# The second feed-forward layer's first product, computed block-wise by Strassen's seven products

## Chip, cores, metric

One core of a Trainium2 chip runs the whole program. The metric is device time in microseconds (us), the median of the runs shown.

## What is computed

Inputs are q, k, v of shape (4, 8, 576, 64) and two pairs of weights, 512 x 2048 and 2048 x 512, all float32. A retention step (attention with a decaying mask) makes 2304 tokens of 512 features; two feed-forward layers follow.

```
scores = scale * q @ k.T;  ret = scores * Dmat;  x = ret @ v        # 2304 x 512
h = x @ w_in;  g = max(h, 0) + log1p(exp(-abs(h)));  x = g @ w_out  # first phase
h = x @ w_in;  r = max(h, 0);  g = r * r;            x = g @ w_out  # second phase
```

## The kernel before

TensorE multiplies float32r operands. To reach float32 precision, each operand is split into a high part (a rounding cast on ScalarE) and a low part (the rest, a subtraction on VectorE), and each product is made of three matmuls: high by high, low by high, high by low.

The tokens are cut into five blocks per phase, of 512 or 384 tokens (`TILES`, `TILES2`, L25 and L26). In a block the loop goes over 16 slices `f` of 128 hidden features. One step of it is: `g1` (L306 to L320), the first product, 12 matmuls that put 128 features by `n` tokens into one of two PSUM tiles `ph`; the nonlinearity on ScalarE and VectorE (`softplus_a` and `softplus_b` in the first phase, `relu2_a` and `relu2_b`, L349 to L358, in the second); `split_g` (L360), the high and low part of the result; and `g2` (L370), the second product, which adds into PSUM tiles `acc` that live for a whole block. `g2` of a step is issued two steps after its `g1` (L512), so the elementwise chain has two steps of TensorE work to hide behind. In the second phase `g2` holds 128 tokens stationary and moves 512 output columns, so it has 9 matmuls per step for 384 tokens and 12 for 512.

Weights arrive as raw 64-bit words, one 512 KB load for each 128-row slice (`load_w`, L100), are put together as float32 on ScalarE (L125, L126) and VectorE (L130) and split into high and low parts (L139, L140). `pump` and `pump_step` issue this work between the steps: the first phase's 32 slices during block 0 (`weights`, L483), the second phase's during the last block of the first phase and the first of the second (L518 to L525). Retention runs chunk by chunk (64 tokens) between the steps of blocks 0 to 3 (`attend`, L469); each chunk is loaded `LOADS` chunks ahead. The output of the first phase goes to DRAM (`x2d`) and is loaded again block by block (`load_x`).

All loads and stores are issued from SyncE's queue. The order on each engine is set by a scheduler at build time, which may issue independent instructions in another order than the code has; only the start (L436 to L463) is written out by hand.

Of the kernel before, what the change touches and what calls it, by code (L numbers as in the profile page):

```python
# [19 lines left out]
SCN = 9  # L20
LOADS = 4
STAGES = 3
EARLY = 8

TILES = ((0, 512), (512, 384), (896, 512), (1408, 512), (1920, 384))  # L25
TILES2 = ((0, 384), (384, 512), (896, 512), (1408, 512), (1920, 384))  # L26

# [7 lines left out]
def kernel(  # L35
# [19 lines left out]


    nc = tc.nc
    NT, DM = out.shape
# [14 lines left out]
    stage = ctx.enter_context(tc.tile_pool(name="stage", bufs=STAGES))  # L73
    cvt = ctx.enter_context(tc.tile_pool(name="cvt", bufs=3))
    xs = ctx.enter_context(tc.tile_pool(name="xs", bufs=1))
# [16 lines left out]
    mask = cst[CN:P, C_MASK:C_MASK + CN].unsqueeze(1).to_broadcast([CN, H, CN])  # L92
    x2d = dram.tile([KD, P, NT], F32, name="x2d")


# [14 lines left out]

    def split_w(phase, kind, f):

        t = staged.pop((kind, f))  # L120
        y, up, low = t.bitcast(F32)[:, :, 1], t[:, :, 1], t[:, :, 0]
        ct = cvt.tile([P, DM], U32, tag="ct", name="ct")
# [12 lines left out]
        y = ct.bitcast(F32)  # L135
        pool = wts if f < EARLY else late_wts[0]
        hi = pool.tile([P, DM], F32R, tag=f"{kind}h{f}", name=f"{kind}h{f}")
        lo = pool.tile([P, DM], F32R, tag=f"{kind}l{f}", name=f"{kind}l{f}")
# [6 lines left out]
    for phase, (wi, wo) in enumerate(((w1_in, w1_out), (w2_in, w2_out))):  # L145
        for f in range(KF + 2):
            if f < KF:
                items.append((phase, wi, "wi", f))
            if f >= 2:
                items.append((phase, wo, "wo", f - 2))  # L150
    n_load = [0]
    n_split = [0]

    def pump_load(upto):
        while n_load[0] < min(upto, len(items)):
            _, src, kind, f = items[n_load[0]]
            load_w(src, kind, f)
            n_load[0] += 1
# [3 lines left out]
    def pump_step():  # L162

        if not splitting:
            m = n_split[0]
            if m == len(items):
                return
            pump_load(m + 1)
            splitting.append(split_w(items[m][0], items[m][2], items[m][3]))
            n_split[0] += 1  # L170
        if next(splitting[0]):
            splitting.clear()
            pump_load(n_split[0] + STAGES)

# [110 lines left out]

    def split_x(raw, phase, n):

        xop.clear()
        for kk in range(KD):
            h, l = x_hi()[:, kk, :n], x_lo()[:, kk, :n]  # L290
            if phase == 0:
                r = raw[:, :n // CN, kk]
                h, l = (a.rearrange("p (m b) -> p m b", b=CN) for a in (h, l))
            else:
                r = raw[:, kk, :n]
            if kk % 2 == 0:
# [8 lines left out]

    def g1(phase, key, f, n):  # L306
        ph = ps_h.tile([P, 512], F32, tag="h", name="ph")
        wh, wl = w_hi[phase, "wi", f], w_lo[phase, "wi", f]
        todo, rest = [], []
# [38 lines left out]

    def relu2_a(key, n):  # L349
        r = ew.tile([P, 512], F32, tag="e", name="r", bufs=3)[:, :n]  # L350
        nc.scalar.activation(out=r, in_=hps.pop(key)[:, :n], func=AF.Relu)  # L351
        tmp[key] = r

    def relu2_b(key, n):
        r = tmp.pop(key)
        g = ew.tile([P, 512], F32, tag="l", name="g")[:, :n]
        nc.vector.tensor_tensor(out=g, in0=r, in1=r, op=ALU.mult)  # L357
        tmp[key] = g  # L358

    def split_g(key, n):  # L360
# [8 lines left out]

    def g2(phase, key, f, n, begin, end):  # L370
        h, l = gg.pop(key)
        wh, wl = w_hi[phase, "wo", f], w_lo[phase, "wo", f]
        n_out = KD if phase == 0 else n // P
        if begin:
            for j in range(n_out):
                acc[j] = ps_acc.tile([P, 512], F32, tag="at", name="acc")
        for j in range(n_out):
            c = slice(j * P, (j + 1) * P)
            if phase == 0:
                o = acc[j][:, :n]  # L380
                todo = [(wh[:, c], h[:, :n]), (wh[:, c], l[:, :n]), (wl[:, c], h[:, :n])]
            else:
                o = acc[j]
                todo = [(h[:, c], wh), (h[:, c], wl), (l[:, c], wh)]
            for m, (a, x) in enumerate(todo):
                nc.tensor.matmul(o, lhsT=a, rhs=x, start=(begin and m == 0), stop=(end and m == 2))  # L386

    def drain(phase, t0, n):
        for j in range(KD if phase == 0 else n // P):
            w = n if phase == 0 else DM  # L390
            if j % 2 == 0:
                o = cvt.tile([P, 512], F32, tag="ct", name="xo")
            else:
                o = ew.tile([P, 512], F32, tag="l", name="xo")
            if j % 2 == 0:
                nc.scalar.copy(o[:, :w], acc[j][:, :w])
            else:
                nc.vector.tensor_copy(o[:, :w], acc[j][:, :w])
            if phase == 0:
                nc.sync.dma_start(out=x2d[j, :, t0:t0 + n], in_=o[:, :w])  # L400
            else:
                nc.sync.dma_start(out=out[t0 + j * P:t0 + (j + 1) * P, :], in_=o)

    def load_x(t0, n):
        raw = xs.tile([P, KD, 512], F32, tag="xr", name="xr")
        nc.sync.dma_start(
            out=raw[:, :, :n], in_=x2d[:, :, t0:t0 + n].rearrange("k p n -> p k n")
        )
        return raw


    blocks = [(0, t0, n) for t0, n in TILES] + [(1, t0, n) for t0, n in TILES2]
    steps = [(b, f) for b in range(len(blocks)) for f in range(KF)]
    last_b = len(TILES) - 1

    need = [(t0 + n) // CN for t0, n in TILES]

    x_next = [None]

# [63 lines left out]
    def weights(j):  # L483

        first = (2, 2, 2, 3)[:j + 1]
        return min(len(items) // 2, 2 + int(sum(first) + 1.9 * (j + 1 - len(first))))

    def run_g2(j):
        b, f = steps[j]
        ph, t0, n = blocks[b]  # L490
        g2(ph, j, f, n, f == 0, f == KF - 1)
        if f == KF - 1:
            drain(ph, t0, n)

    for j, (b, f) in enumerate(steps):
        ph, t0, n = blocks[b]
        g1(ph, j, f, n)
        if ph == 0:
            softplus_a(j, n)
        else:  # L500
            relu2_a(j, n)
        if j == 0:
# [3 lines left out]
        if j >= 1:  # L506
            split_g(j - 1, blocks[steps[j - 1][0]][2])
        if ph == 0:
            pump(max(0, weights(j) - n_split[0]))
        if ph == 0:  # L510
            attend(b, f)
        if j >= 2:  # L512
            run_g2(j - 2)
        if ph == 0:
            softplus_b(j, n)
        else:
            relu2_b(j, n)
        if b in (last_b, last_b + 1):  # L518
            base = f + KF * ph
            goal = len(items) // 2 + max(int(0.6 * (base + 1)), 2 * (base - KF) + 5)  # L520
            while n_split[0] < min(goal, len(items)):
                _, _, kind, wf = items[n_split[0]]
                if wf + (1 if kind == "wi" else 3) > base:
                    break
                pump(1)  # L525
        if f == KF - 1 and b + 1 < len(blocks):
            split_x(x_next[0] if b >= last_b else x_raw.pop(b + 1), *blocks[b + 1][::2])
            if last_b <= b + 1 < len(blocks) - 1:
                x_next[0] = load_x(*blocks[b + 2][1:])
    j = len(steps)  # L530
    split_g(j - 1, blocks[-1][2])
    run_g2(j - 2)
    run_g2(j - 1)


# [73 lines left out]
```

## Time and profile before

| | us |
|---|---|
| median of 3 runs (lowest, highest) | 894.03 (892.5, 896.06) |
| the profiled execution | 897.41 |
| its span in the trace | 895.6 |
| TensorE matmuls busy in that span | 880.3 |
| VectorE busy | 480.0 |
| ScalarE busy | 426.0 |

The profile is of one execution, 3.38 us above the median; 1.8 us of it lie outside the span. Matmul records are modelled to their end and overlap, so matmuls are best priced by the distance between their starts.

### The profile page before, as it was taken

What the parts mean: (1) busy time and instruction counts of PE and PEld (TensorE: products, weight loads), DVE (VectorE), ACT (ScalarE), POOL (GpSimd) and SP (SyncE); (2) the same over time, 40 slices, a digit from 0 to 9 for tenths busy, and PEclk for the clock granted to TensorE, in tenths of its full rate; (3) what the DMA queues carried; (4) which work ended last, traced back from release to release, by engine and by line L of the source; (5) the groups of instructions that cost most, each with busy time, mean ns of one, the idle gap of its engine ahead of it and who ended that gap; (6) DMA issues with size and microseconds to landing.
All of it is one profiled execution on the core that took longest, in us unless ns stands there. A gap on an engine that the chain in (4) does not pass through costs nothing.

```text
span 895.6 us, 13279 instructions
## 1 busy us (share of the span) xinstructions
PE 880.3 (98%) x5462; PEld 756.4 (84%) x5462; DVE 480.0 (54%) x788; ACT 426.0 (48%) x751; POOL 9.6 (1%) x13
## 2 busy tenths in 40 slices
PE   7799999999999999999999999999999999999998
PEld 7677887999888888888999999888888888888997
DVE  2589998666756575556776777322432243223322
ACT  2479997444544444444795697222222222222222
POOL 2100000000000000000000000000000000000000
PEclk9899999999999999999999999999999999999999
DMA  9957674211211112000530673200010011000100
GB/s 226 211 173 222 197 207 132 80 48 48 84 48 48 27 44 71 2 1 2 194 123 1 203 224 103 83 1 0 29 66 1 0 36 48 1 1 0 48 1 36
DMA packets 36012, 68.69 MB, mean 77 GB/s; under 512 B 2928, under 2 KB 21488, under 8 KB 35952
## 3 DMA queue, kind: packets, MB, share of 16 engines
q1 hardware_dynamic: 35952, 67.85, 25.9%
q8 instruction: 43, 0.70, 0.3%
q14 instruction: 17, 0.14, 0.0%
HBM read 58.40 MB, written 9.44 MB: 76 GB/s over the span
## 4 chain that ended last, share of the span: by engine, by line
PE 91%; ACT 3%; DMA 3%; DVE 1%; SPq 1%; issue 0%; POOL 0%
PE ph L317 43%; PE acc L386 43%; PE st L239 3%; PE po L261 2%; DMA ch<-in_kv_dram 1%; DMA cst<-in_consts_dram 1%; DMA wi_raw<-in_moe_w_in_dram 1%; PE st L245 1%; DVE ct L130 0%; ACT wi_raw L126 0%; ACT e L332 0%; ACT woh L139 0%; ACT wi_raw L125 0%; ACT e L331 0%; ACT l L333 0%
## 5 line engine op out<-in xcount | busy, mean ns | idle before, releaser
L317 PE MATMUL ph<-xh,wih 128*128 128x512 f32 (+1 forms) x640 | 238.1, 372 | 1.9 <-ACT wih L139 1.0
L317 PE MATMUL ph<-xh,wil 128*128 128x512 f32 (+1 forms) x640 | 237.8, 372 | 0.0
L317 PE MATMUL ph<-xl,wih 128*128 128x512 f32 (+1 forms) x640 | 158.7, 369 | 0.0
L317 PEld LDWEIGHTS ph<-xh,wih 128*128 128x128 f32 x640 | 121.0, 189 | 20.1 <-ACT wih L139 1.4
L317 PEld LDWEIGHTS ph<-xh,wil 128*128 128x128 f32 x640 | 121.0, 189 | 16.7
L317 PEld LDWEIGHTS ph<-xl,wih 128*128 128x128 f32 x640 | 117.9, 189 | 15.3
L386 PE MATMUL acc<-gh,woh 128*128 128x512 f32 (+1 forms) x320 | 120.5, 376 | 0.0
L386 PE MATMUL acc<-gh,wol 128*128 128x512 f32 (+1 forms) x320 | 117.8, 368 | 0.0
L386 PE MATMUL acc<-gl,woh 128*128 128x512 f32 (+1 forms) x320 | 117.7, 368 | 0.0
L386 PE MATMUL acc<-woh,gl 128*128 128x512 f32 x288 | 112.6, 391 | 0.0
L386 PE MATMUL acc<-wol,gh 128*128 128x512 f32 x288 | 112.6, 391 | 0.0
L357 DVE TENSOR_TENSOR g<-r 128x512 f32<-128x512 f32 (+1 forms) x80 | 50.9, 636 | 114.8 <-ACT r L351 112.0
L386 PE MATMUL acc<-woh,gh 128*128 128x512 f32 x288 | 112.0, 389 | 0.0
L351 ACT ACTIVATE r<-ph 128x512 f32<-128x512 f32 (+1 forms) x80 | 44.2, 552 | 131.1 <-PE ph L317 131.1
L365 DVE TENSOR_TENSOR gl<-g,gh 128x512 fp32r<-128x512 f32 (+1 forms) x80 | 51.0, 638 | 101.7 <-ACT gh L364 101.7
L364 ACT CAST gh<-g 128x512 fp32r<-128x512 f32 (+1 forms) x80 | 46.2, 578 | 113.9 <-PE acc L386 106.7
L364 ACT CAST gh<-e 128x512 fp32r<-128x512 f32 (+1 forms) x80 | 46.1, 576 | 104.8 <-DVE e L344 77.4
L338 DVE SCALAR_TENSOR_TENSOR e<-e 128x512 f32<-128x512 f32 (+1 forms) x80 | 51.0, 638 | 65.5 <-ACT l L333 64.7
L365 DVE TENSOR_TENSOR gl<-e,gh 128x512 fp32r<-128x512 f32 (+1 forms) x80 | 51.0, 637 | 36.5 <-ACT gh L364 36.0
L331 ACT ACTIVATE e<-ph 128x512 f32<-128x512 f32 (+1 forms) x80 | 44.3, 554 | 53.3 <-PE ph L317 52.5
L386 PEld LDWEIGHTS acc<-gh,woh 128*128 128x128 f32 x320 | 60.0, 188 | 8.7
L386 PEld LDWEIGHTS acc<-gh,wol 128*128 128x128 f32 x320 | 60.1, 188 | 7.8
(48 smaller groups left out, 1026.5 us busy)
## 6 DMA issues: line engine op xcount, KB each, us to landing
wi_raw<-in_moe_w_in_dram SPq DMA_DIRECT2D x32, 512.0 KB, 4.6
wo_raw<-in_moe_w_out_dram SPq DMA_DIRECT2D x32, 512.0 KB, 4.2
ch<-in_qk_t_dram SPq DMA_DIRECT2D x36, 256.0 KB, 4.3
ch<-in_kv_dram SPq DMA_DIRECT2D x36, 256.0 KB, 4.7
out_dram<-xo SPq DMA_DIRECT2D x18, 256.0 KB, 2.0
x2d<-xo SPq DMA_DIRECT2D x12, 256.0 KB, 2.3
xr<-x2d SPq DMA_DIRECT2D x3, 1024.0 KB, 5.0
x2d<-xo SPq DMA_DIRECT2D x8, 192.0 KB, 2.0
```

The source lines that it names most:

```text
L239: nc.tensor.matmul(pb[HI, h, :], lhsT=kk[LO, h, :], rhs=qp[LO, h, :], start=True, stop=True, skip_group_check=True,)
L245: nc.tensor.matmul(st[LO, h, :], lhsT=kk[HI, h, :], rhs=sv[HI, h, :], start=c % SCH == 0 and h == 0, stop=True, skip_group_check=True,)
L261: nc.tensor.matmul(po[(LO, HI)[h % 2], h // 2, :], lhsT=sv[rows, h, :], rhs=qp[rows, h, :], start=True, stop=True, skip_group_check=True,)
L317: nc.tensor.matmul(ph[:, :n], lhsT=a, rhs=x, start=(j == 0), stop=(j == len(todo) - 1))
L331: nc.scalar.activation(out=e, in_=ph[:, :n], func=AF.Abs)
L338: nc.vector.scalar_tensor_tensor(out=e, in0=e, scalar=-2.0, in1=e, op0=ALU.add, op1=ALU.mult)
L351: nc.scalar.activation(out=r, in_=hps.pop(key)[:, :n], func=AF.Relu)
L357: nc.vector.tensor_tensor(out=g, in0=r, in1=r, op=ALU.mult)
L364: nc.scalar.copy(h[:, :n], g)
L365: nc.vector.tensor_tensor(out=l[:, :n], in0=g, in1=h[:, :n], op=ALU.subtract)
L386: nc.tensor.matmul(o, lhsT=a, rhs=x, start=(begin and m == 0), stop=(end and m == 2))
```

## The change

The first product of the second phase is no longer computed slice by slice over blocks of 512 or 384 tokens. The weight matrix is taken in pairs of hidden slices (`p` and `p + 8`) and halves of the 512 inner features, which makes a 2 x 2 block matrix A; the tokens are taken in three pairs of 384, which with the inner halves makes a 2 x 2 block matrix B. Strassen's scheme (Winograd's form) gets the four blocks of A B from seven block products instead of eight. Each block product is 6 matmuls of 384 columns. The sums of weight blocks (S) are made once, during blocks 1 to 3 of the first phase, written to DRAM (`s2d`, 8 pairs of 7 operands of 256 KB) and streamed back for each of the three token pairs through five slots (`load_s`). The sums of token blocks (T) are made on VectorE and ScalarE (`build_t`), for the first pair during the last block of the first phase, for the others during the pair before. The products are combined on VectorE from two PSUM buffers (`px`, `py`, `pz` share them). The second product is unchanged in its arithmetic and is cut into pieces of 3 matmuls, which are issued between the block products. `LOADS` goes from 4 to 3 and `cvt` from 3 to 6 buffers. The core of the diff:

```
-LOADS = 4
+LOADS = 3
...
+A11, A12, S2, S4, S3, S1, A22 = range(7)
+PRODUCTS = (A11, S2, A12, S3, S1, A22, S4)
+T_SLOTS = 10
+S_SLOTS = 5
...
+    def store_s(p, first, src):
+        n = src.shape[1] // (KH * P)
+        h, l = (new_ct(F32R)[:, :n * KH * P] for _ in range(2))
+        nc.scalar.copy(h, src)
+        nc.vector.tensor_tensor(out=l, in0=src, in1=h, op=ALU.subtract)
+        for part, o in enumerate((h, l)):
+            nc.sync.dma_start(
+                out=s2d[p, first:first + n, :, part].rearrange("o p c -> p o c"),
+                in_=o.bitcast(F32).rearrange("p (o c) -> p o c", o=n),
+            )
+
+    def split_s(p):
+        cts = []
+        for f in (p, p + NP):
+            t = staged.pop(("wi", f))
+            cts.append(new_ct())
+            yield from words(t, cts[-1])
...
+        store_s(p, A11, top)
+        yield
+        store_s(p, A22, a22)
+        yield
+        nc.vector.tensor_tensor(out=a22, in0=a21, in1=a22, op=ALU.add)
+        nc.vector.tensor_tensor(out=a21, in0=a11, in1=a21, op=ALU.subtract)
+        nc.vector.tensor_tensor(out=a11, in0=a22, in1=a11, op=ALU.subtract)
+        nc.vector.tensor_tensor(out=a12, in0=a12, in1=a11, op=ALU.subtract)
+        yield
+        store_s(p, S3, bot)
+        yield
+        store_s(p, S2, top)
+        yield True
...
+    def build_t(i):
+        k = i % 7
+        if k == 1:
+            nc.vector.tensor_tensor(out=raw(0, 0), in0=raw(0, 1), in1=raw(0, 0), op=ALU.subtract)
+            nc.vector.tensor_tensor(out=t2(), in0=raw(1, 1), in1=raw(0, 0), op=ALU.subtract)
+        elif k == 3:
+            nc.vector.tensor_tensor(out=raw(0, 1), in0=raw(1, 1), in1=raw(0, 1), op=ALU.subtract)
+        elif k == 5:
+            nc.vector.tensor_tensor(out=raw(1, 0), in0=raw(1, 0), in1=t2(), op=ALU.subtract)
+        src = (raw(0, 0), t2(), raw(1, 0), raw(0, 1), raw(0, 0), raw(1, 0), raw(1, 1))[k]
+        t = t_slot(i)
+        nc.scalar.copy(t[:, 0], src)
+        nc.vector.tensor_tensor(out=t[:, 1], in0=src, in1=t[:, 0], op=ALU.subtract)
...
+    def finish(b, p, i, j, c, done=None):
...
+        nc.scalar.copy(h, g)
+        nc.vector.tensor_tensor(out=l, in0=g, in1=h, op=ALU.subtract)
+        for m in range(MH):
+            pieces.append((b, p, i, j, m, (h, l)))
...
+        count = (2, 2, 2, 1, 2, 2, 1)
+        skip = 5
...
+                    if b + 1 < NB and p in (3, 4, 5) and k == 2:
+                        build_t((b + 1) * 7 + p - 3)
+                    if b + 1 < NB and p == NP - 1 and k < 4:
+                        build_t((b + 1) * 7 + 3 + k)
+                    if b == 0 and k in (0, 3):
+                        if n_split[0] < len(items) and not (p >= 4 and k == 3):
+                            pump(1)
+                    load_s((b * NP + p) * 7 + k + 1 + S_SLOTS)
...
+                product(b, p, 0, px, True)
+                nc.scalar.copy(s1, px)
+                after(0)
+                product(b, p, 1, py, True)
+                nc.vector.tensor_tensor(out=u2, in0=s1, in1=py, op=ALU.add)
+                after(1)
+                product(b, p, 2, px, False)
+                nc.scalar.activation(out=r, in_=px, func=AF.Relu)
+                later.append(lambda: finish(b, p, 0, 0, None, r))
+                after(2)
+                product(b, p, 3, py, False)
+                nc.vector.tensor_tensor(out=u3, in0=s1, in1=py, op=ALU.add)
+                after(3)
+                product(b, p, 4, pz, True)
+                c22 = add(u3, pz)
+                later.append(lambda: finish(b, p, 1, 1, c22))
+                after(4)
+                product(b, p, 5, py, False)
+                c21 = add(s1, py)
+                later.append(lambda: finish(b, p, 1, 0, c21))
+                after(5)
+                product(b, p, 6, pz, False)
+                c12 = add(u2, pz)
+                later.append(lambda: finish(b, p, 0, 1, c12))
+                after(6)
...
+        if 1 <= b < last_b:
+            total, i = 9 * NP, (b - 1) * KF + f
+            while n_steps[0] < min(total, -(-total * (i + 1) // (KF * (last_b - 1) - 2))):
+                pump_step()
+                n_steps[0] += 1
+        if b == last_b:
...
+            if f >= 4 and f % 2 == 0:
                 pump(1)
+            for i in range(7):
+                if f == GROUP * (i // 2) + GROUP + 1 + i % 2:
+                    build_t(i)
```

`after(k)` first runs the finish that stands in `later`, then issues `count[k]` pieces, then the extra work shown. `NB` is 3 (token pairs), `NP` 8 (slice pairs), `KH` 2, `MH` 3.

## Rows read from the trace of the kernel before

**Rows 1.** The page's part 4: the chain that ended last, by engine.
```profile
PE 91%; ACT 3%; DMA 3%; DVE 1%; SPq 1%; issue 0%; POOL 0%
```

**Rows 2.** Busy time by stretch: stretch, length, each engine (instructions), PEclk, DMA share, GB/s.
```profile
160.00:424.00 264.00, 264.00 (x1961) 226.51 (x1960) 160.58 (x258) 123.48 (x206) 0.00 (x0) 1.00 0.14 40
424.00:493.00 69.00, 69.00 (x387) 67.20 (x386) 50.44 (x92) 50.87 (x98) 0.00 (x0) 1.00 0.32 104
493.00:560.00 67.00, 67.00 (x344) 61.46 (x343) 50.53 (x87) 51.98 (x97) 0.00 (x0) 1.00 0.56 177
560.00:819.00 259.00, 259.00 (x1144) 214.52 (x1144) 78.50 (x121) 64.49 (x108) 0.00 (x0) 1.00 0.07 23
```

**Rows 3.** The chain in order of time, blocks of 512 tokens: start, us, what.
```profile
571.99 2.72 PE acc L386 x12
574.71 2.72 PE ph L317 x12
```

**Rows 4.** TensorE's timeline, first phase, 384 tokens: start, us, instruction.
```profile
442.09 0.33 PE L317 MATMUL ph<-xh,wih 128*128 128x384 f32 x1
...
444.17 0.33 PE L386 MATMUL acc<-gh,woh 128*128 128x384 f32 x1
```

**Rows 5.** TensorE's timeline, last block of the second phase, around 824 and 841 us.
```profile
824.21 0.33 PE L317 MATMUL ph<-xh,wih 128*128 128x384 f32 x1
...
825.28 0.33 PE L317 MATMUL ph<-xh,wih 128*128 128x384 f32 x1
...
826.32 0.39 PE L386 MATMUL acc<-woh,gh 128*128 128x512 f32 x1
...
827.02 0.39 PE L386 MATMUL acc<-woh,gh 128*128 128x512 f32 x1
...
827.71 0.39 PE L386 MATMUL acc<-woh,gh 128*128 128x512 f32 x1
...
841.64 0.33 PE L317 MATMUL ph<-xh,wih 128*128 128x384 f32 x1
...
845.83 0.33 PE L317 MATMUL ph<-xh,wih 128*128 128x384 f32 x1
```

**Rows 6.** Groups by line and shape: busy us, mean ns; idle before and releaser.
```profile
L344 DVE SCALAR_TENSOR_TENSOR e<-ph,l 128x384 f32<-128x384 f32 x32 | 17.8, 556 | 0.9
L365 DVE TENSOR_TENSOR gl<-g,gh 128x384 fp32r<-128x384 f32 x32 | 17.8, 556 | 23.7 <-ACT gh L364 23.7
L365 DVE TENSOR_TENSOR gl<-g,gh 128x512 fp32r<-128x512 f32 x48 | 33.2, 692 | 78.0 <-ACT gh L364 78.0
L364 ACT CAST gh<-g 128x384 fp32r<-128x384 f32 x32 | 16.3, 509 | 24.9 <-PE acc L386 22.9 <-DVE g L357 2.0
L364 ACT CAST gh<-g 128x512 fp32r<-128x512 f32 x48 | 29.9, 624 | 89.0 <-PE acc L386 83.8 <-DVE g L357 5.1
L125 ACT ACTIVATE wi_raw<-wi_raw 128x512 f32<-128x512 f32 x32 | 21.6, 674 | 3.4 <-DMA wi_raw<-in_moe_w_in_dram 3.4
L126 ACT ACTIVATE wi_raw<-wi_raw,cst 128x512 uint32<-128x512 uint16 x32 | 24.4, 763 | 0.0
L130 DVE SCALAR_TENSOR_TENSOR ct<-wi_raw 128x512 uint32<-128x512 uint32 x32 | 22.9, 715 | 0.7 <-ACT wi_raw L126 0.5
```

**Rows 7.** The page's part 6: a DMA issue of 256 KB, median us to landing.
```profile
ch<-in_kv_dram SPq DMA_DIRECT2D x36, 256.0 KB, 4.7
```

**Rows 8.** SyncE's timeline: start, us, one DMA issue.
```profile
0.73 0.56 SPq L210 DMA_DIRECT2D ch<-in_qk_t_dram  x1
```

**Rows 9.** VectorE's timeline: an instruction with the idle time before it and its releaser.
```profile
474.18 0.56 DVE L365 TENSOR_TENSOR gl<-e,gh 128x384 fp32r<-128x384 f32 x1 [0.64 <-ACT gh L364]
```

**Rows 10.** ScalarE's timeline, last block of the first phase, weights among the steps.
```profile
456.61 0.69 ACT L125 ACTIVATE wo_raw<-wo_raw 128x512 f32<-128x512 f32 x1
...
457.82 0.49 ACT L331 ACTIVATE e<-ph 128x384 f32<-128x384 f32 x1
458.20 0.68 ACT L125 ACTIVATE wi_raw<-wi_raw 128x512 f32<-128x512 f32 x1
458.75 0.54 ACT L332 ACTIVATE e<-e 128x384 f32<-128x384 f32 x1
```

More of the change, by code (lines that the diff above doesn't have):

```diff
@@ L142, in split_w @@
         yield True
-    items = []
[L145 to L150, printed above, removed]
+    def store_s(p, first, src):
[7 more added lines that the diff above has]
+                in_=o.bitcast(F32).rearrange("p (o c) -> p o c", o=n),
+            )
@@ L151 @@
+    for p in range(2, NP):
+        order += [p + NP] + ([p + 2] if p < NP - 2 else [])
+    for f in order:
+        items.append((1, split_w, (1, "wo", f)))
+        loads.append((w2_out, "wo", f))
     n_load = [0]
     n_split = [0]
+    n_used = [0]
     def pump_load(upto):
-        while n_load[0] < min(upto, len(items)):
-            _, src, kind, f = items[n_load[0]]
-            load_w(src, kind, f)
+        while n_load[0] < min(upto, len(loads)):
+            load_w(*loads[n_load[0]])
@@ L290, in split_x @@
             h, l = x_hi()[:, kk, :n], x_lo()[:, kk, :n]
[L291 to L295, printed above, removed]
+            r = raw[:, :n // CN, kk]
+            h, l = (a.rearrange("p (m b) -> p m b", b=CN) for a in (h, l))
             if kk % 2 == 0:
@@ L404, in load_x @@
[L404 to L413, printed above, removed]
+            todo = [(wh[:, c], h[:, :n]), (wh[:, c], l[:, :n]), (wl[:, c], h[:, :n])]
+            for m, (a, x) in enumerate(todo):
+                nc.tensor.matmul(
+                    acc[j][:, :n], lhsT=a, rhs=x, start=(begin and m == 0), stop=(end and m == 2)
+                )
@@ new lines, in drain_one, with drain @@
+    def drain_one(j, src, dst, n):
+        if j % 2 == 0:
+            o = cvt.tile([P, 512], F32, tag="ct", name="xo")[:, :n]
+            nc.scalar.copy(o, src[:, :n])
+        else:
+            o = ew.tile([P, 512], F32, tag="l", name="xo")[:, :n]
+            nc.vector.tensor_copy(o, src[:, :n])
+        nc.sync.dma_start(out=dst, in_=o)
+    def drain(t0, n):
+        for j in range(KD):
+            drain_one(j, acc[j], x2d[j, :, t0:t0 + n], n)
+    NB = NT // PAIR
+    MH = HALF // P
+    mem = {}
@@ new lines, in product @@
+    def product(b, p, k, ps, first):
+        w = s_slot((b * NP + p) * 7 + k)
+        t = t_slot(b * 7 + k)
+        todo = []
+        for kk in range(KH):
+            c = slice(kk * P, (kk + 1) * P)
+            todo += [(w[:, 0, c], t[:, 0, kk]), (w[:, 1, c], t[:, 0, kk]), (w[:, 0, c], t[:, 1, kk])]
+        for m, (a, x) in enumerate(todo):
+            nc.tensor.matmul(
+                ps, lhsT=a, rhs=x, start=(first and m == 0), stop=(m == len(todo) - 1),
+                skip_group_check=True,
+            )
@@ new lines, with piece @@
+    pieces = []
+    acc2 = {}
+    def piece(b, p, i, j, m, g):
+        h, l = g
+        f = p + i * NP
+        wh, wl = w_hi[1, "wo", f], w_lo[1, "wo", f]
+        begin, end = p == 0 and i == j, p == NP - 1 and i != j
+        if begin:
+            pool, tag = (((ps_acc, "at"),) * 4 + ((ps_at, "at"), (ps_st, "st")))[j * MH + m]
+            acc2[j, m] = pool.tile([P, 512], F32, tag=tag, name="acc")
+        c = slice(m * P, (m + 1) * P)
+        for n, (a, x) in enumerate([(h[:, c], wh), (h[:, c], wl), (l[:, c], wh)]):
+            nc.tensor.matmul(
+                acc2[j, m], lhsT=a, rhs=x, start=(begin and n == 0), stop=(end and n == 2)
+            )
+        if end:
+            t0 = b * PAIR + j * HALF + m * P
+            drain_one(j * MH + m, acc2[j, m], out[t0:t0 + P, :], DM)
```

250 lines of the change are left out of this document (164 added, 86 removed).

## The prediction

> **What bounds the kernel now.** I read the chain of work that ended last first, then busy time by stretch, then TensorE's timeline, and only then the durations of the other engines. The chain is TensorE's for 91% of the span [rows 1], and from 160 to 819 us TensorE is busy in every microsecond of each stretch, at a granted clock of 1.00, the 2.4 GHz level [rows 2]. So time is the number of matmuls times the distance between their starts, and other engines count only where they make TensorE wait. The reader should see in the timeline that this distance is not one number. In blocks of 512 tokens twelve matmuls take 2.72 us, 226.7 ns each [rows 3]. In the first phase's blocks of 384 tokens, where nothing else is in the stream, twelve take 444.17 - 442.09 = 2.08 us, 173.3 ns each [rows 4]. Where matmuls of 384 and of 512 columns alternate, both get dearer after each change of size [rows 5]: the first six of 384 columns take 825.28 - 824.21 = 1.07 us (178 ns each), the first six of 512 take 827.71 - 826.32 = 1.39 us (232 ns), the first three 827.02 - 826.32 = 0.70 us.
>
> **TensorE, before.** The second phase has 48 steps with 512 tokens (12 + 12 matmuls, 2 x 2.72 us, 261.1 us in all) and 32 steps with 384 tokens (12 of 384 columns, 9 of 512). One such step takes 845.83 - 841.64 = 4.19 us [rows 5], so 134.1 us. Together 395.2 us.
>
> **TensorE, after.** The first product has 3 token pairs x 8 slice pairs x 7 products x 6 matmuls = 1008 matmuls of 384 columns in place of 576 of 512 and 384 of 384: seven eighths of the columns. The second product keeps its 864 matmuls of 512 columns, in 12 pieces of three per slice pair. The order is product, two pieces (at two places one), product, and so on: runs of six and six, or six and three, so each run lies wholly in the dear part after a change of size. Per slice pair: 7 x 1.07 + 5 x 1.39 + 2 x 0.70 = 15.84 us, and 24 of them make 380.2 us. **Term: -15.0 us.** The bounds are the undisturbed distances, 1008 x 173.3 + 864 x 226.7 ns = 370.6 us (-24.6), and on the other side a full penalty per change of size as the long runs show it: 7 x (2.11 - 2.08 + 2.76 - 2.72), that is 0.5 us per slice pair, with 2.11 us as 826.32 - 824.21 and 2.76 us as 12 matmuls at 230 ns, so 382 us (-13). I take the short runs because they copy the new order.
>
> A page rule bears on this. The Trainium skill, page "TensorE: Matmul & The Clock Gate", section "Back-to-back issue gap", gives an isolated distance of columns / 2.4 GHz + 2.5 ns at the full clock, which depends on the columns alone: by it (an estimate) 162.5 and 215.8 ns, 373.2 us before and 350.3 us after, a gain of 22.9 us. The trace disagrees: 226.7 ns undisturbed [rows 3], more after a change.
>
> **Weight sums in blocks 1 to 3 (added).** Per slice pair ScalarE gets two raw conversions (2 x (0.674 + 0.763) us) and four casts (three of 512 columns at 0.624, one of 256 at about 0.40, drawn down the line from 0.624 at 512 and 0.509 at 384): 5.1 us. VectorE gets 2 x 0.715, three subtractions at 0.692, one of 256 and four sums of 256 columns at about 0.42 each (same line, 0.692 and 0.556): 5.6 us [rows 6]. Eight pairs: ScalarE +41, VectorE +45 us in a stretch of 264 us in which they are busy 123 and 161 [rows 2]; they go to 62% and 78%. The cover is the lag of two steps between first and second product, some 8 to 11 us of TensorE, against an elementwise chain of some 4 us. SyncE issues 64 stores and 16 raw loads more there, 0.56 us each [rows 8]; chunk loads queue behind stores that wait for VectorE. Bytes: 14.7 MB of sums and 8.4 MB of raw weights, +88 GB/s on 40, below the 177 GB/s at which TensorE never paused [rows 2]. **I take +1 us**, bounds 0 and 4 (a late chunk costs about one landing, 4.7 us [rows 7]). `LOADS` 3 instead of 4 leaves two chunk distances of some 8 us or more for a landing of 4.7 us: nothing, unless the queue holds it up, which that bound covers.
>
> **Last block of the first phase (moved).** It loses some 9 weight splits and gets 6 splits (the last half of the weights moves to the first token pair) and 7 builds of T: 7 casts and 11 subtractions of 768 columns, about 0.85 and 0.96 us by the slopes between 384 and 512 columns [rows 6]. Net: VectorE 10.6 - 3 x 1.41 = +6.4 us, ScalarE 6.0 - 3 x 2.06 = about 0, on 50 and 51 of 69 us [rows 2]. The same stretch now hides a comparable load with TensorE fully busy, since the engines' queues mix the weights' instructions among the step's own [rows 10]. **+1 us**, bounds 0 and 5.
>
> **Second phase, VectorE and ScalarE (added).** Per slice pair VectorE has 13 instructions of 384 columns at 0.556 us (7.2 us), ScalarE 6 at about 0.51 (3.1), in 15.84 us: about half and a fifth. What can stop TensorE is the return of a PSUM buffer: two buffers serve `px`, `py`, `pz`, and a product that adds into one waits for the reader of what it held. The shortest way from a product's end to the next use is one piece, a product and two pieces: 0.70 + 1.07 + 1.39 = 3.16 us. A reader that finds VectorE free needs 0.56 us plus a handoff of about 0.13 (0.64 us of waiting around a cast of 0.51 [rows 9]). Ahead of it stands at most the previous finish: result, cast, low part, 0.556 + 0.64 + 0.556 = 1.75 us. Sum 2.4 us: covered. A piece needs its operands some 6 us after they are begun (five older pieces and two or three products lie between), the chain takes about 3: covered.
>
> Extra work breaks this cover. At the second T of a pair (product 2 of slice pair 4) two subtractions, a cast and a low part (0.96 + 0.96 + 0.85 + 0.13 + 0.96 = 3.9 us) can stand between the finish and the next reader: 1.75 + 3.9 + 0.69 = 6.3 us after product 2 ends, while the reader itself became possible 2.5 us and the buffer is due 5.6 us after that end: a wait of some 0.7 to 1.5 us. In the last slice pair four builds lie in a row: some 0.5 us. Two changes of token pair give 2.4 to 4. The ten weight splits in the first pair (VectorE 1.41, ScalarE 2.06 us each) just fit when I lay them out, since a gap of 2.4 us without reader stands behind each. **+3 us**; bounds 0, and 24 items (14 builds, 10 splits) x 1.5 = 36.
>
> **The S stream (added).** 168 loads of 256 KB, 44 MB in 380 us, 116 GB/s more, under the 177 above. A slot is loaded after its product and needed five products later: four products and at least eight pieces, 4 x 1.07 + 8 x 0.70 = 9.8 us; issue and landing take 0.56 + 4.7 = 5.3 us [rows 7, 8]. Nothing on the path; if SyncE is held by a store that waits, up to 4.5 us are in hand. Start and tail keep their chain (last pieces, copies, stores): nothing.
>
> **Sum.** -15.0 + 1 + 1 + 3 = -10 us. Against the profiled execution, 897.4, that is 887.4; that one lies 3.4 us above the median of the runs shown, so the forecast for the median is 894.0 - 10 = **884.0 us**.
>
> **Rivals.** *Undisturbed distances:* size changes in short, regular runs cost nothing, 370.6 us; with the same 5 us of waits 874.4. For it: long runs fall back to the undisturbed distance; against: every change of size in rows 5 shows the penalty. By the Trainium skill's rule cited above, which knows no neighbours, it would land beside this. Chance 0.17, its own range 869 to 879.
> *Slower, by the two product buffers:* VectorE's queue holds a reader behind extra work, and product 3, 5 or 6 waits at its first matmul. It costs 1 us at each of the 24 items: -15 + 2 + 24 = +11, 905 us. It turns to slower (over 4.5 us) when the items cost 0.8 us on average. For it: VectorE waits on ScalarE in each finish, in order; against: the scheduler mixes queues [rows 10], and half of the load is free. Chance 0.20.
> *No change:* the same waits at 0.3 to 0.7 us per item plus the first phase's bounds eat 10 to 19 us: 890 to 898, about 894. Chance 0.18.
> That the change doesn't save the columns can be left out: the loop counts fix it.
>
> **How the numbers follow.** The forecast has 0.45, own range 879 to 889. Within 0.5% means within 4.5 us, about what a measurement of this kernel can tell from no change. Faster: 0.45 + 0.17 = 0.62; same 0.18; slower 0.20. The range goes from 871, a part of the undisturbed case, to 903, into the slower case; about 0.07 lies below and 0.11 above.
>
> **What would show it.** Right: in the second phase about 178 ns between matmuls of 384 columns and 232 of 512, 15.8 us per slice pair, gaps of about a microsecond only where T is built. Wrong: 173 and 227 ns (undisturbed); first matmuls of a product that wait for VectorE in most slice pairs (slower); any wait for S; TensorE idle in blocks 1 to 3.

## The result, and the profile after

The changed kernel takes **878.12 us** (median of 4 runs, 877.78 to 879.94) against 893.87 us for the kernel before in the same comparison (4 runs, 892.5 to 896.06): ratio 0.9826, 95% interval 0.9802 to 0.985, a gain of 15.75 us where the forecast had 10. The profiled execution took 877.78 us, its span is 876.0 us and its mean granted clock 0.993.

The page of the kernel after: the chain that ended last, by engine, and the loads of the sums of weights (S).

```profile
PE 81%; DMA 7%; DVE 5%; ACT 5%; issue 1%; SPq 1%; POOL 0%; DVEq 0%; ACTq 0%
...
sring<-s2d SPq DMA_DIRECT2D x168, 256.0 KB, 2.7
```

TensorE's share of the chain was 91% [rows 1]. That is a share of a chain and not time lost: behind a short wait the chain can stay on other engines for long. What TensorE lost of it lies nearly all in the first phase; in the last block the chain in order of time (start, us, what) has:

```profile
432.08 5.04 DMA wo_raw<-in_moe_w_out_dram
...
437.15 0.68 ACT wo_raw L141
```

A load of raw weights and its conversion on ScalarE lie on the path there, to a wait of TensorE of 0.4 us at 444 us.

Busy time by stretch of the kernel after, columns as in [rows 2].

```profile
160.00:424.00 264.00, 264.00 (x1942) 226.58 (x1941) 192.47 (x330) 153.44 (x266) 0.00 (x0) 1.00 0.44 133
424.00:493.00 69.00, 67.79 (x380) 65.62 (x379) 57.83 (x97) 51.01 (x97) 0.00 (x0) 1.00 0.30 97
493.00:560.00 67.00, 66.71 (x338) 60.43 (x338) 40.91 (x76) 26.25 (x50) 0.00 (x0) 1.00 0.57 179
560.00:819.00 259.00, 259.00 (x1290) 232.77 (x1289) 136.91 (x239) 60.52 (x115) 0.00 (x0) 1.00 0.48 136
```

Against [rows 2], TensorE is still busy in every microsecond from 160 to 424 us (blocks 1 to 3 without the first 20 us or so of block 1) and of the second phase from 560 to 819, while VectorE went from 161 to 192 us and from 79 to 137. So the added work lies beside TensorE there. In these stretches only the last block of the first phase (424 to 493) and the entry to the second phase lost something: 1.2 and 0.3 us without a matmul.

TensorE's timeline of the kernel after, one slice pair of the second phase (start, us, instruction, how many).

```profile
505.02 1.22 PE L546 MATMUL px<-t,sring 128*128 128x384 f32 x6
506.08 0.39 PE L565 MATMUL acc<-woh,gh 128*128 128x512 f32 x1
...
507.47 1.21 PE L546 MATMUL py<-t,sring 128*128 128x384 f32 x6
508.52 0.39 PE L565 MATMUL acc<-woh,gh 128*128 128x512 f32 x1
...
513.38 0.39 PE L565 MATMUL acc<-woh,gring 128*128 128x512 f32 x1
...
514.08 1.22 PE L546 MATMUL pz<-t,sring 128*128 128x384 f32 x6
515.14 0.39 PE L565 MATMUL acc<-woh,gring 128*128 128x512 f32 x1
...
520.71 0.51 PE L546 MATMUL px<-t,sring 128*128 128x384 f32 x2
...
850.13 1.22 PE L546 MATMUL px<-t,sring 128*128 128x384 f32 x6
```

From the first product of one slice pair to that of the next are 520.71 - 505.02 = 15.69 us; the forecast had 15.84. Six matmuls of 512 columns take 507.47 - 506.08 = 1.39 us and three 514.08 - 513.38 = 0.70, as priced. Six of 384 take 508.52 - 507.47 = 1.05 us behind six of 512, and 515.14 - 514.08 = 1.06 behind three; 1.07 was priced. All seven together take 15.69 - 5 x 1.39 - 2 x 0.70 = 7.34 us, 1.05 each. The last line is the first product of the last slice pair: (850.13 - 505.02) / 22 = 15.69 us, and each of the 22 distances is 15.69, those with builds of T and weight splits among them.

**Where the 19.6 us between the two spans (895.6 and 876.0) came from.** Three places of TensorE's timelines serve as marks; in each pair of times the first is of the kernel before, the second of the kernel after. Block 1 of the first phase, with which the weight sums begin, starts at 141.21 and 137.38 us, its last block at 424.01 and 420.58, the second phase at 492.67 and 490.85.

TensorE's timeline of the kernel before at the three marks.

```profile
141.21 0.33 PE L317 MATMUL ph<-xh,wih 128*128 128x384 f32 x1
...
424.01 0.33 PE L317 MATMUL ph<-xh,wih 128*128 128x384 f32 x1
...
492.67 0.33 PE L317 MATMUL ph<-xh,wih 128*128 128x384 f32 x1
```

And of the kernel after.

```profile
137.38 1.31 PE L402 MATMUL ph<-xh,wi 128*128 128x384 f32 x6
...
420.58 1.57 PE L402 MATMUL ph<-xh,wi 128*128 128x384 f32 x8
...
490.85 1.25 PE L546 MATMUL px<-t,sring 128*128 128x384 f32 x6
```

The lead is 3.83 us at the first mark, 3.43 at the second, 1.82 at the third. So blocks 1 to 3 cost 0.4 us, the last block cost 1.6 us, and the second phase brought the rest: 19.6 - 1.8 = 17.8 us. The 0.4 us lie in block 1, since block 2 begins at 225.27 and 221.84 us, again 3.43 apart. The 3.8 us that were there before block 1 begins are scatter of the start. The run with six blocks of 384 tokens, told of below, has the first phase of the kernel before, and its block 1 begins 4.4 us sooner than in the profiled execution of before. TensorE's timeline of that run:

```profile
136.76 0.33 PE L317 MATMUL ph<-xh,wih 128*128 128x384 f32 x1
```

In the kernel after and the seven runs that share its start and its first blocks, block 1 begins between 136.0 and 138.5 us. Without the 3.8 us the spans differ by 15.8 us, as the medians do (15.75).

What stopped TensorE after the start shows in its waits (engine, line, waited for: us in total, times, longest), kernel after.

```profile
PE ph L402 <- DVE e L429: 3.0, 5, 1.5
...
PE ph L402 <- DVE xh L384: 1.1, 1, 1.1
...
PE py L546 <- DVE uring L653: 0.3, 1, 0.3
```

Three of the five waits of the first line, 1.2 us together, lie in the last block. The second line is at the start of block 1, for VectorE's rounding of the block's tokens; the kernel before waits 0.3 us there. The third is the only wait of the second phase for a product buffer, at 500.7 us. Where T of the next token pair is built there is none. VectorE's timeline of the kernel after shows both: a step of the last block, and the last slice pair of the first token pair.

```profile
475.25 0.55 DVE L423 SCALAR_TENSOR_TENSOR e<-e 128x384 f32<-128x384 f32 x1
475.71 0.69 DVE L175 TENSOR_TENSOR wol<-ct,woh 128x512 fp32r<-128x512 f32 x1
476.32 0.55 DVE L426 SCALAR_TENSOR_TENSOR l<-e,l 128x384 f32<-128x384 f32 x1
476.79 0.95 DVE L526 TENSOR_TENSOR raw<-raw 128x768 f32<-128x768 f32 x1
477.65 0.55 DVE L429 SCALAR_TENSOR_TENSOR e<-ph,l 128x384 f32<-128x384 f32 x1
...
611.50 0.95 DVE L526 TENSOR_TENSOR raw<-raw 128x768 f32<-128x768 f32 x1
612.37 0.55 DVE L592 TENSOR_TENSOR gl<-g,gh 128x384 fp32r<-128x384 f32 x1
612.84 0.55 DVE L636 TENSOR_TENSOR c<-uring,py 128x384 f32<-128x384 f32 x1
613.35 0.96 DVE L527 TENSOR_TENSOR raw<-raw 128x768 f32<-128x768 f32 x1
```

In the first phase a weight split (L175) and a part of a T build (L526) stand between the three instructions of one step's chain and make it longer, and TensorE waits for its end (L429 reads the PSUM tile `ph` that TensorE is to write next). In the second phase the builds (768 columns) don't stand together either: a part of a finish (L592) and a reader of `py` (L636) lie between the two subtractions, so the reader has one build instruction ahead of it and not four. The forecast had laid them out by hand in code order.

### The profile page after: what moved, and what is told of

The parts are those of the page before. It is cut to its first block, busy times and chain, and to the rows that moved or that the text cites. A ratio compares the mean times of both kernels' runs of the same rounds, so it can differ in the third digit from the quotient of the medians.

```text
span 876.0 us, 14182 instructions
## 1 busy us (share of the span) xinstructions
PE 857.5 (98%) x5510; PEld 753.6 (86%) x5510; DVE 577.0 (66%) x992; ACT 422.1 (48%) x761; POOL 10.3 (1%) x13
## 4 chain that ended last, share of the span: by engine, by line
PE 81%; DMA 7%; DVE 5%; ACT 5%; issue 1%; SPq 1%; POOL 0%; DVEq 0%; ACTq 0%
PE acc L565 23%; PE ph L402 17%; PE acc L454 17%; PE py L546 8%; PE px L546 6%; PE pz L546 6%; PE st L327 2%; DMA ch<-in_kv_dram 2%; DMA wo_raw<-in_moe_w_out_dram 2%; PE po L349 2%; DMA wi_raw<-in_moe_w_in_dram 2%; DVE ct L146 1%; DMA cst<-in_consts_dram 1%; PE st L333 1%; DVE e L423 1%
## 5 line engine op out<-in xcount | busy, mean ns | idle before, releaser
L402 PE MATMUL ph<-xh,wi 128*128 128x512 f32 (+1 forms) x640 | 148.7, 374 | 5.5 <-DVE e L429 3.0
L402 PEld LDWEIGHTS ph<-xh,wi 128*128 128x128 f32 x640 | 117.4, 190 | 24.4 <-DVE e L429 2.8
L565 PE MATMUL acc<-woh,gring 128*128 128x512 f32 x288 | 104.9, 393 | 0.0
L546 PE MATMUL py<-t,sring 128*128 128x384 f32 x432 | 86.9, 335 | 0.3 <-DVE uring L653 0.3
L546 PEld LDWEIGHTS py<-t,sring 128*128 128x128 f32 x432 | 77.2, 188 | 6.8 <-DVE uring L653 0.6
L402 PE MATMUL ph<-xl,wi 128*128 128x512 f32 (+1 forms) x320 | 79.3, 369 | 0.0
L591 ACT CAST gh<-g 128x384 fp32r<-128x384 f32 x48 | 24.6, 513 | 86.8 <-DVE g L578 72.1
L454 PEld LDWEIGHTS acc<-gl,woh 128*128 128x128 f32 x320 | 60.1, 188 | 7.3 <-DVE gl L439 0.2
L402 PEld LDWEIGHTS ph<-xl,wi 128*128 128x128 f32 x320 | 59.0, 189 | 7.8
L591 ACT CAST gring<-g 128x384 fp32r<-128x384 f32 x48 | 24.6, 513 | 83.2 <-DVE g L578 83.2
L546 PE MATMUL px<-t,sring 128*128 128x384 f32 x288 | 58.3, 337 | 0.0
L546 PE MATMUL pz<-t,sring 128*128 128x384 f32 x288 | 58.2, 337 | 0.0
```

What stands on the lines that cost most here:

```text
L402: nc.tensor.matmul(ph[:, :n], lhsT=a, rhs=x, start=(j == 0), stop=(j == len(todo) - 1))
L454: nc.tensor.matmul(acc[j][:, :n], lhsT=a, rhs=x, start=(begin and m == 0), stop=(end and m == 2))
L546: nc.tensor.matmul(ps, lhsT=a, rhs=x, start=(first and m == 0), stop=(m == len(todo) - 1), skip_group_check=True,)
L565: nc.tensor.matmul(acc2[j, m], lhsT=a, rhs=x, start=(begin and n == 0), stop=(end and n == 2))
L591: nc.scalar.copy(h, g)
```

## The experiments

All ratios are to the kernel before, run on the same chip in the same comparison (medians 893.75 and 893.81 us). Differences to the kernel after go across comparisons; the medians of the kernel before lie within 0.12 us of one another in all three.

**Is an item of TensorE's stream still paid in full?** Product 1 is computed twice in every slice pair; the second computation overwrites the first.

```diff
                 product(b, p, 1, py, True)
+                product(b, p, 1, py, True)
```

> Edit: product 1 of every slice pair is computed twice into the same buffer, the second time over the first, so there are eight block products again (1152 matmuls of 384 columns); the result is the same. Theory (the second phase is matmul starts, everything else is covered): a second run of six directly behind the first costs 6 x 173.3 ns = 1.04 us, 24 times, +25.0 us, 878.1 + 25 = 903 us, slower than the kernel before by 9 us, because blocks of 384 columns pay more per column than blocks of 512. Rival (VectorE or the stream of S operands sets the pace of a slice pair): the added TensorE work fills waits, +0 to +12 us, 878 to 890.

Measured: 903.28 us (900.87 to 903.79), ratio 1.0091, interval 1.0063 to 1.012. That is 25.2 us more than the kernel after for 24 x 6 matmuls, 1.05 us for six. TensorE's timeline of this run, the doubled product:

```profile
609.40 2.25 PE L546 MATMUL py<-t,sring 128*128 128x384 f32 x12
611.48 0.39 PE L565 MATMUL acc<-woh,gh 128*128 128x512 f32 x1
```

Twelve take 611.48 - 609.40 = 2.08 us, the undisturbed distance of [rows 4]. The second phase is bound by the number of matmuls, and with eight products in place of seven the change would be slower than the kernel before.

**Does the size of the matmul, not the algorithm, make part of the difference?** The kernel before with six blocks of 384 tokens in its second phase.

```diff
-TILES2 = ((0, 384), (384, 512), (896, 512), (1408, 512), (1920, 384))
+TILES2 = tuple((384 * i, 384) for i in range(6))
```

> Edit, on the kernel before: the second phase in six blocks of 384 tokens, without Strassen. It separates the two sides of the change. Theory (distances of the rows before): 96 steps of 4.19 us in place of 395.2 us, 402.2, so +7.0 us, 901 us. Rival (the penalty of a change of size was a matter of those two blocks alone, and the rest runs at 173.3 and 226.7 ns): 96 x 4.12 = 395.5 us, +0.3 us, 894 us.

Measured: 899.99 us (899.15 to 902.35), ratio 1.0066, interval 1.0044 to 1.0087: 6.2 us slower than before. Alternating 384 and 512 columns costs what [rows 5] say, so the change has to win this back first: against this run it gains 899.99 - 878.12 = 21.9 us, of which the kernel before, with its undisturbed blocks of 512, had 6 already. The run with the doubled product, where the eighth product costs 25.2 us, has the same second-phase matmuls as this one (1152 of 384 columns and 864 of 512). It took 3.3 us more, with intervals that overlap, so what the scheme costs beside its matmuls these two runs don't settle.

**Do the builds of T cost nothing, or is their cost hidden in the sum?** The builds for the second and third token pair are left out, and their products use the first pair's T, so their part of the output is that of the first pair.

```diff
-        t = t_slot(b * 7 + k)
+        t = t_slot(k)
...
-                    if b + 1 < NB and p in (3, 4, 5) and k == 2:
-                        build_t((b + 1) * 7 + p - 3)
-                    if b + 1 < NB and p == NP - 1 and k < 4:
-                        build_t((b + 1) * 7 + 3 + k)
```

> Edit: the T operands of the second and third token pair are left out, their products read those of the first pair (so their part of the result is that of the first pair's tokens); 14 casts on ScalarE and 22 subtractions on VectorE go. Theory (the builds are covered): 878 us, within 0.7 us, and the clump of work on VectorE around 611 to 620 us is gone without a change in the distances of TensorE's matmuls. Rival (the forecast's term: each change of token pair costs 1.2 to 2 us): 874 to 876 us.

Measured: 877.35 us (876.14 to 877.71), ratio 0.9805, interval 0.9782 to 0.9829. That is 0.8 us below the kernel after, inside the overlap of the intervals; the forecast's 2.4 to 4 us for these builds is not there to be taken away. The traces agree: from the second slice pair to the last every distance is 15.69 us in both kernels. What the run shows beside it: the entry wait at 500 us is 1.43 us here in place of 0.29, although no build stands near it. VectorE stands 1.05 us before the `g` of the first finish (L583, at 499.00 us), until a store of `xo` is done; the next experiment shows why. In the kernel after VectorE does not stop there, and output copies and weight splits lie ahead of the reader.

**Is it the scheduler's mixing that keeps them free?** The second phase is issued in code order on every engine.

```diff
-    second_phase([lambda: g2_parts(j - 2), lambda: g2_parts(j - 1)])
+    with tc.manual_schedule():
+        second_phase([lambda: g2_parts(j - 2), lambda: g2_parts(j - 1)])
```

> Edit: every engine takes the second phase's instructions in the order of the code, the scheduler does not mix them. Theory 1 (the builds cost nothing because the scheduler mixes them among the chain of each product): the waits of the forecast appear, 2.4 to 4 us at the two changes of token pair and some at the ten weight splits, 880.5 to 884 us, with TensorE waiting for readers of the product buffers. Theory 2 (the cover is larger than the forecast laid out, whatever the order): 878 us, within 0.7 us.

Measured: 886.71 us (883.87 to 890.63), ratio 0.9906, interval 0.9877 to 0.9935, 8.6 us above the kernel after. TensorE's timeline of this run, from 505 us, the matmuls with the longest idle times before them (in brackets, with what ended them), and what followed the first:

```profile
505.22 2.29 PE L546 MATMUL py<-t,sring 128*128 128x384 f32 x6 [4.55 <-DVE uring L653]
507.30 0.63 PE L565 MATMUL acc<-woh,gh 128*128 128x512 f32 x1
...
509.86 0.52 PE L546 MATMUL pz<-t,sring 128*128 128x384 f32 x1
...
571.52 1.31 PE L546 MATMUL py<-t,sring 128*128 128x384 f32 x6 [0.92 <-DVE uring L653]
...
638.21 1.28 PE L546 MATMUL pz<-t,sring 128*128 128x384 f32 x6 [1.05 <-DMA sring<-s2d]
...
641.89 1.33 PE L546 MATMUL px<-t,sring 128*128 128x384 f32 x6 [1.70 <-DVE c L636]
```

At 701.64 us stands the same wait as at 571.52, 0.92 us. VectorE's timeline of the same run, before the wait at 571 us and at two others:

```profile
503.00 0.56 DVE L583 TENSOR_TENSOR g<-r 128x384 f32<-128x384 f32 x1 [4.86 <-DMA x2d<-xo]
...
567.20 0.95 DVE L526 TENSOR_TENSOR raw<-raw 128x768 f32<-128x768 f32 x1
568.18 0.96 DVE L527 TENSOR_TENSOR raw<-raw 128x768 f32<-128x768 f32 x1
570.04 0.96 DVE L535 TENSOR_TENSOR t<-raw,t 128x768 fp32r<-128x768 f32 x1 [0.91 <-ACT t L534]
570.92 0.55 DVE L653 TENSOR_TENSOR uring<-uring,py 128x384 f32<-128x384 f32 x1
...
638.83 0.56 DVE L578 SCALAR_TENSOR_TENSOR g<-c 128x384 f32<-128x384 f32 x1 [4.90 <-DMA out_dram<-xo]
```

Lines 567 to 571 are the forecast's layout for the second T of a pair: two subtractions, the wait for ScalarE's cast, the low part, and only then the reader of `py`. TensorE stands still for 0.9 us there at both changes of token pair, and the slice pair takes 16.87 us, 1.2 more than the others, inside the 0.7 to 1.5 of the forecast; the last slice pair, with four builds in a row, takes 0.2 us more. So the mechanism is right, 2.7 us for both changes where 2.4 to 4 were forecast, and the kernel after avoids it through its order. The rest was in neither theory. (The profiled execution is the slowest of the six, 890.63 us; its span is 12.9 us above that of the kernel after: 6.6 in the first slice pair, 3.2 in the ninth, around 638 us, 2.7 at the changes of token pair.) In code order VectorE also stands 4.9 us before a `g` of a finish, because `g` and the output copy `xo` share a tag of two buffers and the older one is still being stored. Behind the second such stand, which ends at 638.83, a product waits 1.7 us; another waits 1.05 us for S there. The first, which ends at 503.00, stops TensorE for 4.6 us, and after it six matmuls of 384 columns take 507.30 - 505.22 = 2.08 us, twice the usual time. Busy time by stretch shows the granted clock, in the column after the engines: 0.50, the lower of the two levels (1.2 GHz), for the five microseconds behind the pause.

```profile
505.00:510.00 5.00, 4.78 (x13) 4.20 (x14) 3.46 (x7) 1.45 (x3) 0.00 (x0) 0.50 1.04 363
```

**Would more work on VectorE matter?** The low part of every finish and the sums `u2` and `u3` are computed twice, 6 instructions or, by their listed durations, 3.3 us of VectorE per slice pair.

```diff
         nc.vector.tensor_tensor(out=l, in0=g, in1=h, op=ALU.subtract)
+        nc.vector.tensor_tensor(out=l, in0=g, in1=h, op=ALU.subtract)
...
                 nc.vector.tensor_tensor(out=u2, in0=s1, in1=py, op=ALU.add)
+                nc.vector.tensor_tensor(out=u2, in0=s1, in1=py, op=ALU.add)
...
                 nc.vector.tensor_tensor(out=u3, in0=s1, in1=py, op=ALU.add)
+                nc.vector.tensor_tensor(out=u3, in0=s1, in1=py, op=ALU.add)
```

> Edit: six of VectorE's thirteen instructions of a slice pair (four low parts of the results, u2 and u3) are issued twice, with the same operands; the result is the same. +3.3 us of VectorE per slice pair of 15.7 us. Theory (the way back of the product buffers has room, VectorE busy about 53% there): 878 us, at most +1 us. Rival (the slower rival of the forecast: each reader that comes later makes a product wait): +0.3 us and more per product, 168 products, 920 us or more.

Measured: 878.65 us (878.11 to 879.3), ratio 0.9831, interval 0.9813 to 0.9849. Its busy time by stretch:

```profile
560.00:819.00 259.00, 259.00 (x1290) 232.76 (x1289) 182.44 (x337) 59.86 (x115) 0.00 (x0) 1.00 0.44 136
```

VectorE goes from 137 to 182 of 259 us, 70%, and TensorE misses nothing. The product buffers have that much in hand; the rival of the slow buffers is refuted with a margin, for work that the scheduler may place.

**How much has the S stream in hand?** Two S slots in place of five.

```diff
-S_SLOTS = 5
+S_SLOTS = 2
```

> Edit: two slots instead of five for the streamed S operands, so a load is issued when its slot's product ends and needed after one product and three or four pieces, 3.1 or 3.8 us. By the landing time measured in the changed kernel, 2.7 us, with 0.45 us of issue and a handoff: 3.2 to 3.4 us, waits of 0.1 to 0.3 us at four of seven products, 10 to 30 us in all, 888 to 908 us. By the forecast's price (0.56 + 4.7 us): waits of 1.5 to 2.2 us at every product, +250 us or more.

Measured: 890.65 us (888.56 to 895.46), ratio 0.9972, interval 0.9952 to 0.9991, 12.5 us above the kernel after. TensorE's longest wait for S:

```profile
631.42 2.22 PE L546 MATMUL pz<-t,sring 128*128 128x384 f32 x6 [2.10 <-DMA sring<-s2d]
```

A slot is then loaded after its product and needed two products later, one product and some pieces on. With the 5.3 us that the forecast took for issue and landing this would be some 250 us slower; with a landing of 2.6 us (the page's median for this run) most loads are in time. Six products of 168 show a wait for S, 5.6 us together. The rest of the 12.5 us is only in part accounted for: at the entry to the second phase a piece waits 1.5 us for ScalarE, and the granted clock is 0.66 on average from 501 to 506 and from 631 to 636 us, where the kernel after has 1.00. So the forecast's 4.7 us [rows 7], which belong to the first phase's chunk loads, was too long for S, and its reserve of five slots is larger than it said.

**Can the waits of the last first-phase block go?** The 11 subtractions of the first pair's T builds are done by GpSimd, which is idle there.

```diff
     def build_t(i):
+        eng = nc.gpsimd if i < 7 else nc.vector
...
-        nc.vector.tensor_tensor(out=t[:, 1], in0=src, in1=t[:, 0], op=ALU.subtract)
+        eng.tensor_tensor(out=t[:, 1], in0=src, in1=t[:, 0], op=ALU.subtract)
```

(and so for the four other subtractions of the function)

> Edit: the eleven subtractions of the seven T builds in the last block of the first phase run on GpSimd instead of VectorE. Theory (the 1.6 us that this block lost are VectorE's queue: a PSUM tile of the first product is read too late): TensorE's waits for line 429 in 424 to 493 us go, -1 to -1.6 us, 876.5 to 877 us. Rival (GpSimd is too slow or hinders VectorE there, or the waits come from the weight splits): 878 us or more.

Measured: 892.39 us (888.74 to 894.07), ratio 0.9976, interval 0.9961 to 0.9991. A miss: 14 us slower than the kernel after where a gain of about one was expected. GpSimd's timeline of this run:

```profile
436.52 2.17 POOL L527 TENSOR_TENSOR raw<-raw 128x768 f32<-128x768 f32 x1
438.77 2.00 POOL L528 TENSOR_TENSOR raw<-raw 128x768 f32<-128x768 f32 x1
```

and VectorE's in the same microseconds:

```profile
436.91 2.19 DVE L423 SCALAR_TENSOR_TENSOR e<-e 128x384 f32<-128x384 f32 x1
439.14 2.04 DVE L426 SCALAR_TENSOR_TENSOR l<-e,l 128x384 f32<-128x384 f32 x1
...
443.33 0.55 DVE L429 SCALAR_TENSOR_TENSOR e<-ph,l 128x384 f32<-128x384 f32 x1
```

Instructions that take 0.56 us alone take as long as the GpSimd instruction beside them; the one that has `ph`, which lies in PSUM, among its inputs takes 0.55 with a GpSimd instruction running. A step's elementwise chain becomes some 5 us longer (with a conversion of weights in the queue that is slowed as well), and TensorE waits for it four times in this block, 10.5 us together, and has a granted clock of 0.94 from 424 to 493 us where the kernel after had 1.00. The Trainium skill, page "SBUF — State Buffer", section "Who interferes with whom", has the rule: the two engines share one pair of SBUF ports, which is an exclusive lock; a VectorE instruction with two inputs in SBUF contends with a GpSimd instruction that reads SBUF. These rows agree. The move has a second price: GpSimd takes 1.9 to 2.3 us for a subtraction that takes VectorE 0.96, and ScalarE stands 3.7 us before a cast of T (at 440.80 us) until one of these subtractions is done. What each price is alone no run shows.

**A better order of pieces?** The last product of a slice pair gets no piece behind it, the fourth gets two: six runs of six in place of five runs of six and two of three, thus one change of size fewer each way.

```diff
-        count = (2, 2, 2, 1, 2, 2, 1)
+        count = (2, 2, 2, 2, 2, 2, 0)
```

> Edit: the pieces between the products are dealt as (2, 2, 2, 2, 2, 2, 0) instead of (2, 2, 2, 1, 2, 2, 1), so the last product of a slice pair and the first of the next stand side by side. Theory (distances of the changed kernel: 1.389 us for six of 512 columns, 1.044 for six of 384 behind six of 512, 2.084 for twelve in a row): 6 x 1.389 + 5 x 1.044 + 2.084 = 15.64 us per slice pair in place of 15.69, -1.2 us, 877 us. Rival (the shorter way back of a product buffer, 2.4 us in place of 3.2, makes the next product wait): +0.3 us or more at each of 24 slice pairs, 885 us or more.

Measured: 876.96 us (875.92 to 878.78), ratio 0.9814, interval 0.9795 to 0.9833. TensorE's timeline of this run, two slice pairs:

```profile
520.65 1.20 PE L546 MATMUL px<-t,sring 128*128 128x384 f32 x6
...
536.29 0.51 PE L546 MATMUL px<-t,sring 128*128 128x384 f32 x2
```

A slice pair takes 15.64 us, 0.05 less than in the kernel after, and 24 x 0.05 = 1.2 us is what the median gained. It is the fastest version that was run. Its interval overlaps that of the kernel after, so that the trace's period, not the time alone, carries the claim.

## Why the prediction was right, and where its sizes were off

The sign, the bound and the order of the gain came out as argued; the result lies inside the range, though 0.9 us below the likeliest case's own range and inside that of the rival with undisturbed distances (869 to 879). The range of 32 us also held the no-change case and reached into the slower one, so the time alone says little; the steps say more. Of the four terms one was too cheap by 0.6 us and the others too dear by 6.6 together, so the right sign does not come from errors that cancel. Step by step:

- **TensorE, -15.0 us: right in kind, too small.** Measured were 24 x 15.69 = 376.6 us against the 395.2 of before, -18.6. The prices for 512 columns held to 0.01 us. The step that failed is "six of 384 columns take 1.07 us": that was read behind twelve of 512 [rows 5], and behind six of 512 it is 1.05. 0.15 us per slice pair, 3.6 us in all, is the larger part of the miss. By the prediction's own signs the outcome is mixed: 175 ns between matmuls of 384 columns (178 for right, 173 for undisturbed) and 232 of 512 (232 and 227). The bound of undisturbed distances (-24.6) was not reached either: the runs of 512 keep 232 ns. The rule of the Trainium skill that the prediction weighed (page "TensorE: Matmul & The Clock Gate", section "Back-to-back issue gap") made the gain 22.9 us, an estimate from 162.5 and 215.8 ns; the rows speak against it, with 175 and 232 ns. Why six of 384 lose next to nothing in these short runs while those behind three of 512 columns cost 0.01 to 0.02 us more, no run settles.
- **Weight sums in blocks 1 to 3, +1 us: 0.4 us, at the start of block 1.** The lead over before goes from 3.83 to 3.43 us. The wait there is not the late chunk that the forecast named but the rounding of the block's tokens, and whether the weight sums are its cause no run shows. The stretch that the forecast read [rows 2] begins some 20 us into block 1. In it the named cover holds (VectorE 73%, ScalarE 58% busy; 78 and 62 were forecast), and so do 133 GB/s.
- **Last block of the first phase, +1 us: 1.6 us.** The mechanism is the forecast's: builds and splits stand ahead of a step's chain, three times with a wait; on VectorE as priced, and once behind a raw weight's load and conversion on ScalarE, which the forecast had at no cost. VectorE's busy time grew by 7.4 us there and ScalarE's by 0.1; 6.4 and about 0 were forecast.
- **Builds and splits in the second phase, +3 us: 0.6 us, all of it at the entry.** There a product starts 500.74 - 499.24 = 1.50 us behind the one before it, where six matmuls of 384 columns take 1.04, and then takes 501.89 - 500.74 = 1.15. The failed step is the layout by hand at the second T of a pair and in the last slice pair. In code order it happens as priced (1.2 us longer at 571 and at 701 us); in the kernel after the scheduler puts readers and parts of a finish between the builds. The prediction had read this mixing in [rows 10] and used it for the first phase, but not for this term. The entry wait, on the other hand, it did not see.
- **S stream and `LOADS`, 0: right.** No wait for S in the kernel after, on a landing of 2.7 us rather than 4.7.
- **Sum.** -18.6 + 0.4 + 1.6 + 0.6 = -16.0 us. From the start of the last matmul to the end of the span are 4.3 us, 4.1 before, which makes it -15.8: the 19.6 us between the spans without the 3.8 of the start, and 15.75 us between the medians.
- **The rivals.** Undisturbed distances would have given 874.4 us; the distances are not those. Slower by the product buffers fell with the doubled VectorE work (+0.5 us); it needs an order that keeps extra work together. No change needed 0.3 us or more at each of 24 items; none of them shows any, since every distance from the second slice pair on is 15.69 us.

What stays open: why the distances between matmuls lie where they do, and how the loss of 1.6 us in the last block could be avoided, since the one attempt moved the work to an engine that holds VectorE up.

## What to carry to other kernels

When TensorE is busy in every microsecond, price a change by the distance between matmul starts in the very neighbourhood that the new order makes (which size, behind how many of the other), and get that distance from runs of the same length where the trace has any. Lay the other engines' queues out as the scheduler will mix them before charging waits: the same instructions cost nothing here when mixed and 1.2 us a time when they stood together. Before moving elementwise work to an idle GpSimd, look at whether the VectorE instructions beside it read two operands from SBUF.

## What the runs showed of the hardware beyond that

- While GpSimd ran a subtraction of 768 columns (2.0 to 2.2 us), VectorE's instructions with both inputs in SBUF took 2.04 and 2.19 us in place of 0.56; one with an input in PSUM kept 0.55.
- After TensorE stood still for 4.6 us its granted clock was 0.50 for some five microseconds (six of 384 columns in 2.08 us, the next six of 512 in 509.86 - 507.30 = 2.56 us in place of 1.39, the six of 384 behind them in 511.18 - 509.86 = 1.32), so the pause cost about half of its own length again: 2.08 - 1.05 + 2.56 - 1.39 + 1.32 - 1.05 = 2.5 us.
- A load of 256 KB of S landed in 2.7 us while the queue carried 136 GB/s, against 4.7 us for the chunk loads of equal size [rows 7].
- VectorE's listed durations hold some overlap: independent instructions of 384 columns listed with 0.55 us start 0.47 us apart (612.37 and 612.84 in the timeline above).
